# A fused cosine attention and FFN: first loads and head preparation in a hand-chosen order, permuted token order, W3 transposes two ahead

## The chip, the cores and the metric

The kernel runs on one core of a Trainium2 chip. The metric is the device time of one execution in microseconds (us). A profile's span, from the first to the last instruction, is 1.7 to 2.5 us shorter than the time of the same execution.

## The reference, cut to what matters

Eight batches, twelve heads, 448 tokens, head size 64. q and k are divided by their norms, the scores by tau = 0.1, then softmax and the product with v. The result, 3584 x 768, goes through an FFN.

```python
q_n = q / (np.linalg.norm(q, axis=-1, keepdims=True) + 1e-06)
k_n = k / (np.linalg.norm(k, axis=-1, keepdims=True) + 1e-06)
scores = np.matmul(q_n, k_n.transpose(0, 1, 3, 2)) / tau
...                                    # softmax, then attn @ v
h = (x @ w1) * (x @ w2) @ w3
return (h @ w_out)
```

The kernel computes W34 = W3 @ W_out once, for which W3 is transposed on TensorE ("w3t" groups), and then needs only (x W1 * x W2) W34.

## The kernel before

Heads are prepared in groups of six (three pairs). A step t is half a pair: scores and exponentials of pair t/2, attention times v of the pair before, and "filler" groups of FFN matmuls that keep TensorE full. The program order is kept on each engine (in the trace before, the first scaling, whose norms were ready at 8.2 us, stands on POOL until 22.04 behind a load's issue that waited 9.27). In the code `nc.vector` is DVE, `nc.gpsimd` POOL, `nc.scalar` ACT, `nc.tensor` PE. In the profile `raw` is q and k as loaded, `sq` their squares, `ss` the sums of squares, `rt` and `rn` the norm and its reciprocal, `nrm` the scaled q and k, `qkT` (or `qT`, `kT`) their transposes, `sc` the scores. An a-group or b-group is the six matmuls of one block of x W1 or x W2, whose input is `xT`.

```python
def prep_sq(g, i, eng):            # squares, 112x512 for q and for k of pair i
    ...
def prep_sum(g, i):                # nc.vector.reduce_sum, for q and for k
    ...
def prep_rn(g, i0=0, i1=GP):       # rn = 1 / (sqrt(ss) + eps)
    ...
    nc.vector.tensor_scalar_max(t, ss, TINY)
    nc.scalar.activation(t, t, ACT.Ln)
    nc.scalar.activation(t, t, ACT.Exp, scale=0.5)
    nc.vector.tensor_scalar_add(t, t, NORM_EPS)
    nc.vector.reciprocal(rns[g][:, :, sl, :, 0], t)

def tr(pp):
    ...                            # eight transposes into one PSUM tile
    nc.vector.tensor_copy(kts[pp], ps[:, 1, :S])
    nc.vector.tensor_copy(qts[pp].rearrange("p (t j) -> p j t", j=NJ),
                          ps[:, 0, :S].rearrange("p (j t) -> p j t", j=NJ))
...
load_qk(0, 0, 2); load_qk(0, 2, GH); load_v(0); load_w(w3_sb, moe_w3)   # lines joined
load_qk(1); load_w(wo_sb, moe_w_out); load_v(1)
load_w(w1_sb, moe_w1); load_w(w2_sb, moe_w2); load_qk(2)      # all on nc.gpsimd, with a cast
prep_sq(0, 0, nc.vector); prep_sum(0, 0); prep_rn(0, 0, 1); prep_scale(0, 0, nc.gpsimd)
tr(0)
...
def prep_step(s, g):               # steady state: s = step within the group
    ...                            # loads two and three groups ahead, V copy on nc.gpsimd
    n = g + 2
    if n < NG:
        if s < GP:           prep_sq(n, s, nc.gpsimd)
        if 1 <= s <= GP:     prep_sum(n, s - 1)
        if s == GP + 1:      prep_rn(n)
    n = g + 1
    if n < NG and s >= GP:   prep_scale(n, s - GP, nc.gpsimd)

fill += [w3t_group(fo) for fo in range(KO2)]
fill += [w34_group(fo, mh) for fo in range(KO2) for mh in range(2)]
for t in range(2 * NP + 5):
    pp, half = divmod(t, 2)
    scores(pp, half)
    ...                            # trback(pp - 2) in even steps, tr(pp + 1) in odd ones
    if pp >= 1: filler()
    av(pp - 1, half)
    if pp >= 1: filler()
    prep_step(s, g)
```

## Time and profile before

| | before |
|---|---|
| time, median (lowest to highest) | 451.69 us (451.24 to 451.75, four runs; the profiled one 450.96) |
| span of the profiled run | 448.6 us |
| PE busy | 389.9 us |
| first scores | 26.23 us |
| end of the last copy to the end | 445.1 to 448.6 us |

In the page's list of groups the columns are: line, engine, operation, output and input, count, then busy time, mean ns of one, and the idle time before with its releaser. These rows carry the preparation and the two copies that the change merges:

```profile
L121 POOL TENSOR_TENSOR sq<-raw 112x512 bf16<-112x512 bf16 x90 | 91.5, 1041 | 55.3 <-DVE ss L128 47.7
L146 POOL TENSOR_TENSOR nrm<-raw,rn 112x512 bf16<-112x512 bf16 x96 | 96.8, 1044 | 44.4 <-DVE rn L140 44.4
L166 DVE COPY qT<-ps_tr 128x448 bf16<-128x448 bf16 x48 | 55.2, 1150 | 0.0
L165 DVE COPY kT<-ps_tr 128x448 bf16<-128x448 bf16 x48 | 17.7, 368 | 30.8 <-PE ps_tr L159 30.8
```

Squares and scalings are nearly all on POOL. POOL's squares wait 47.7 us in all for VectorE's sums to free their buffers. Even so POOL has long rows in the first 100 us, one of them the seven instructions that will matter below (four squares, V copy, two squares). A max of VectorE's falls into it and takes 2.02 us, where the max has a median of 0.18:

```profile
83.36 4.03 POOL L121 TENSOR_TENSOR sq<-raw 112x512 bf16<-112x512 bf16 x4
87.34 1.46 POOL L109 COPY v_sb<-vraw 112x1536 bf16<-112x1536 bf16 x1
87.82 2.02 DVE L136 TENSOR_SCALAR rt<-ss 112x48 f32<-112x48 f32 x1
88.76 2.03 POOL L121 TENSOR_TENSOR sq<-raw 112x512 bf16<-112x512 bf16 x2
```

### The profile page before, as it was taken

Reading aid. Unit: us, or ns where it says so; the run is one execution under the profiler, and the core shown is the slowest. Engines: PE = TensorE matmul, PEld = TensorE weight load, DVE = VectorE, ACT = ScalarE, POOL = GpSimd, SP = SyncE. Lnnn points to the kernel's source line nnn. Section 1 sums busy time; section 2 is a strip of 40 time slices with the busy share of each in tenths; the row PEclk is TensorE's granted clock in tenths of the full one; section 3 lists DMA queues with packets and bytes.
Section 4 is the critical chain, followed back from the end, with each engine's and each line's share of the span. In section 5 each row is a group of like instructions: output and inputs, shape, how many; then the busy total and the mean of one; then the engine's idle time right before and its main releaser. Section 6 shows DMA issues by size and latency. Waiting matters only on the chain.

```text
span 448.6 us, 9291 instructions
## 1 busy us (share of the span) xinstructions
PE 389.9 (87%) x3904; PEld 228.6 (51%) x3904; DVE 276.6 (62%) x605; ACT 215.8 (48%) x319; POOL 253.6 (57%) x265
## 2 busy tenths in 40 slices
PE   0030579989999999999998999999989999999996
PEld 0010456655555555655565556555655565556553
DVE  2055397877685868576858685768576855564321
ACT  1011334345655565556556655565566555554121
POOL 9148499986767676757676767576747150000000
PEclk9999879999999999999999999999999999999999
DMA  8999916715062706280718071907130011001003
GB/s 108 208 207 213 200 16 91 94 15 81 4 92 77 122 4 91 82 154 2 94 72 129 0 94 72 164 1 94 72 67 1 1 72 72 1 1 72 35 1 140
DMA packets 40776, 34.92 MB, mean 78 GB/s; under 512 B 1312, under 2 KB 34592, under 8 KB 40736
## 3 DMA queue, kind: packets, MB, share of 16 engines
q0 software_dynamic: 36704, 23.33, 37.1%
q1 hardware_dynamic: 4032, 11.01, 6.4%
q8 instruction: 30, 0.49, 0.5%
q14 instruction: 10, 0.08, 0.1%
HBM read 46.66 MB, written 11.01 MB: 129 GB/s over the span
## 4 chain that ended last, share of the span: by engine, by line
PE 80%; DMA 10%; DVE 7%; POOL 1%; issue 0%; ACT 0%; POOLq 0%; ACTq 0%
PE ps_o L220 16%; PE ps_b L220 16%; PE ps_a L220 16%; PE ps_av L193 10%; PE sc L177 10%; DMA raw<-in_k_dram 7%; PE ps_tr L159 5%; PE ps_w L220 4%; DMA w_sb<-in_moe_w_dram 4%; PE ps_tb L211 3%; DVE ss L128 2%; DVE qT L166 1%; DVE w3t_sb L227 1%; DVE osd L202 1%; POOL raw L98 1%; DVE rt L136 1%
## 5 line engine op out<-in xcount | busy, mean ns | idle before, releaser
L184 ACT ACTIVATE expT<-sc 112x896 bf16<-112x896 f32 x192 | 165.4, 914 | 99.6 <-PE sc L177 99.6
L121 POOL TENSOR_TENSOR sq<-raw 112x512 bf16<-112x512 bf16 x90 | 91.5, 1041 | 55.3 <-DVE ss L128 47.7
L146 POOL TENSOR_TENSOR nrm<-raw,rn 112x512 bf16<-112x512 bf16 x96 | 96.8, 1044 | 44.4 <-DVE rn L140 44.4
L220 PEld LDWEIGHTS <-w_sb 128*128 128x128 bf16 x768 | 68.6, 97 | 49.9
L220 PE MATMUL ps_a<-xT,w_sb 128*128 128x448 bf16 x384 | 83.8, 352 | 0.6 <-DVE xT L214 0.3
L220 PE MATMUL ps_b<-xT,w_sb 128*128 128x448 bf16 x384 | 83.1, 352 | 0.0
L220 PE MATMUL ps_o<-w_sb,abT 128*128 128x384 bf16 x448 | 80.8, 326 | 0.0
L177 PE MATMUL sc<-qT,kT 64*112 64x448 bf16 x384 | 58.2, 380 | 23.7 <-DVE qT L166 16.3
L193 PEld LDWEIGHTS <-expT 112*128 112x128 bf16 x1536 | 62.9, 99 | 15.8 <-issue 1.7
L128 DVE TENSOR_REDUCE ss<-sq 112x8 f32<-112x512 bf16 x96 | 61.3, 677 | 14.6 <-POOL sq L121 14.6
L193 PE MATMUL ps_av<-v_sb,expT 112*128 112x65 bf16 x1536 | 66.2, 195 | 0.0
L258 DVE TENSOR_TENSOR abT<-a_sb,ps_b 128x448 bf16<-128x448 bf16 x64 | 39.7, 621 | 37.1 <-PE ps_b L220 34.4
L166 DVE COPY qT<-ps_tr 128x448 bf16<-128x448 bf16 x48 | 55.2, 1150 | 0.0
L220 PEld LDWEIGHTS <-abT 128*128 128x128 bf16 x448 | 41.0, 98 | 23.3 <-issue 0.3
L159 PE MATMUL ps_tr<-ident,nrm 112*128 112x112 bf16 x384 | 28.3, 217 | 23.6 <-POOL nrm L146 23.6
L177 PEld LDWEIGHTS <-kT 64*112 64x112 bf16 x384 | 17.9, 127 | 56.5 <-issue 24.0
L202 DVE TENSOR_TENSOR osd<-ps_av,rs 128x256 bf16<-128x256 f32 x96 | 40.7, 424 | 3.8
L247 ACT CAST a_sb<-ps_a 128x448 bf16<-128x448 f32 x64 | 34.1, 534 | 17.5 <-PE ps_a L220 15.5
L159 PEld LDWEIGHTS <-nrm 112*128 112x128 bf16 x384 | 20.1, 99 | 40.0 <-POOL nrm L146 24.7
L275 ACT COPY out_sb<-ps_o 128x384 f32<-128x384 f32 x28 | 13.4, 479 | 54.4 <-PE ps_o L220 54.4
L165 DVE COPY kT<-ps_tr 128x448 bf16<-128x448 bf16 x48 | 17.7, 368 | 30.8 <-PE ps_tr L159 30.8
L201 DVE RECIPROCAL rs<-ps_av 128x4 f32<-128x4 f32 x96 | 17.7, 185 | 25.7 <-PE ps_av L193 25.7
(30 smaller groups left out, 222.9 us busy)
## 6 DMA issues: line engine op xcount, KB each, us to landing
out_dram<-out_sb SPq DMA_DIRECT2D x28, 384.0 KB, 2.3
vraw<-in_v_dram POOLq DMA_DIRECT2D x16, 336.0 KB, 7.3
raw<-in_q_dram POOLq DMA_DIRECT2D x15, 336.0 KB, 5.0
raw<-in_k_dram POOLq DMA_DIRECT2D x15, 336.0 KB, 6.8
w_sb<-in_moe_w_dram POOLq DMA_DIRECT2D x2, 1536.0 KB, 35.1
w_sb<-in_moe_w_dram POOLq DMA_DIRECT2D x1, 2048.0 KB, 15.7
wo_sb<-in_moe_w_out_dram POOLq DMA_DIRECT2D x1, 1536.0 KB, 24.3
raw<-in_q_dram POOLq DMA_DIRECT2D x1, 224.0 KB, 4.8
```

What stands on the lines that cost most here:

```text
L121: eng.tensor_mul(s.rearrange("p h j d -> p (h j d)"), x, x)
L128: nc.vector.reduce_sum(sss[g][:, t, 2 * i:2 * i + 2, :], sqs.pop((g, i, t)), axis=AX.X)
L146: eng.tensor_mul(nrms[g][:, i, t].rearrange("p j h d -> p h j d"), raws[g][:, t, 2 * i:2 * i + 2], rns[g][:, t, 2 * i:2 * i + 2].to_broadc ...
L159: nc.tensor.transpose(ps[:, t, j * P:(j + 1) * P], n[:, i, t, j].rearrange("p h d -> p (h d)"), ident[:P, :P])
L166: nc.vector.tensor_copy(qts[pp].rearrange("p (t j) -> p j t", j=NJ), ps[:, 0, :S].rearrange("p (j t) -> p j t", j=NJ))
L177: nc.tensor.matmul(sc[:P, hh, :S], kts[pp][64 * hh:64 * hh + 64, c * P:(c + 1) * P], qts[pp][64 * hh:64 * hh + 64, :], start=True, stop=True)
L184: nc.scalar.activation(exps[pp][:, c], sc[:P, :, :S], ACT.Exp, scale=1.0 / float(tau))
L193: nc.tensor.matmul(ps[:, m, :], exps[pp][:, c, hh, q0:q0 + 128], vt[:, 2 * i + hh, c, :], start=(c == 0), stop=(c == NJ - 1))
L202: nc.vector.tensor_mul(osds[pp][:, :, hh, :], ps[:, :, :D], rs.to_broadcast([128, NJ, D]))
L220: nc.tensor.matmul(o, l, r, start=(i == 0), stop=(i == len(pairs) - 1))
L247: nc.scalar.copy(a_sbs[b, fo], ps[:, :S])
L258: nc.vector.tensor_mul(abts[b // 2][:, fo, c0:c0 + S], a_sbs.pop((b, fo)), ps[:, :S])
```

## The change

Its intent is to start TensorE earlier and to take work off VectorE. The first pair's q and k come as fp32 through the SP and ACT queues; the loads stand in one order; groups 0 to 3 are prepared in hand-placed steps, spread over VectorE, ScalarE and GpSimd; steps 0 to 4 have no fillers, step 5 has ten; token order stays permuted until the stores; a W3 transpose is issued two groups ahead of its use. The buffer of W3 is also used again for the FFN's product. Cut to the core:

```diff
-        nc.vector.tensor_copy(kts[pp], ps[:, 1, :S])
-        nc.vector.tensor_copy(
-            qts[pp].rearrange("p (t j) -> p j t", j=NJ),
-            ps[:, 0, :S].rearrange("p (j t) -> p j t", j=NJ))
+        qks[pp] = head_pool.tile([128, 2, S], BF16, tag="qkT", name="qkT")
+        nc.vector.tensor_copy(qks[pp], ps[:, :, :S])
...
+            nc.sync.dma_start(out=out_v[2 * bb + bj // NJ, bj % NJ, p0:p0 + n],
+                              in_=o[r0:r0 + n])          # up to two stores a block
...
+    nc.sync.dma_start(out=raw0[:, 0], in_=q[0, 0:2]...)    # fp32
+    nc.scalar.dma_start(out=raw0[:, 1], in_=k[0, 0:2]...)
...
+    load_qk(0, 2, GH)
...
+    load_w(w3_sb, moe_w3, 0, KO2 // 2)
+    load_v(0)
+    load_w(wo_sb, moe_w_out, 0, KO2)
+    load_qk(1); load_v(1)
...
+    load_w(w3_sb, moe_w3, KO2 // 2, KO2)
+    load_w(w1_sb, moe_w1, 0, KO1)
...
+    fill += [w3t_group(0), w3t_group(1)]
+    for fo in range(KO2):
+        fill.append(w34_group(fo, 0))
+        if fo + 2 < KO2:
+            fill.append(w3t_group(fo + 2))
+        fill.append(w34_group(fo, 1))
+    NFILL0 = 10
...
+        if t == 4:
+            prep_sq(1, 0, 0, DVE);  prep_sq(1, 0, 1, DVE)
+            prep_sq(1, 1, 0, POOL); prep_sq(1, 1, 1, POOL)
+            prep_sum(1, 0, 0); prep_sum(1, 0, 1)
+            prep_max(1, 0, 1); prep_root(1, 0, 1); prep_rn(1, 0, 1)
+            prep_scale(1, 0, 0, DVE); prep_scale(1, 0, 1, DVE)
+        if t == 5:
+            prep_sq(1, 2, 0, POOL); prep_sq(1, 2, 1, POOL)
+            spread_v(1)
+        if t == 6:
+            ...                        # four sums, max, root, rn, then scalings on POOL
...                                    # group 2 in steps 9 to 11, group 3 in 12 to 14
+        if t == 5:
+            av(1, 1)
+            filler(NFILL0)
```

More of the change, by code (lines that the diff above doesn't have):

```diff
@@ L62 @@
     xpool = ctx.enter_context(tc.tile_pool(name="xt", bufs=2))
-    ab_pool = ctx.enter_context(tc.tile_pool(name="ab", bufs=2))
+    ab_pool = ctx.enter_context(tc.tile_pool(name="ab", bufs=1))
     opool = ctx.enter_context(tc.tile_pool(name="opool", bufs=3))
@@ L69 @@
     psM = ctx.enter_context(tc.tile_pool(name="psM", bufs=2, space=PSUM))
-    nc.scalar.preload_act_table_set("natural_log_exp_and_others")
-    ident = const.tile([128, 128], BF16)
-    make_identity(nc, ident)
     w1_sb = wpool.tile([128, KO1, DF], BF16, name="w1_sb")
@@ L78 @@
     w34_sb = wpool.tile([128, KO2, DM], BF16, name="w34_sb")
-    w3_sb = wpool.tile([128, KO2, DF], BF16, name="w3_sb")
     w3t_sb = wpool.tile([128, KO2, DF], BF16, name="w3t_sb")
     wo_sb = wpool.tile([128, KO2, DM], BF16, name="wo_sb")
+    w3_sb = ab_pool.tile([128, KO2, DF], BF16, tag="big", name="w3_sb")
     NV = 3
     v_tiles = [wpool.tile([P, GH, NJ, D + 1], BF16, name=f"v{i}_sb") for i in range(NV)]
-    for t in v_tiles:
-        nc.gpsimd.memset(t[:, :, :, D:D + 1], 1.0)
     raws, vraws, nrms, rns, sss = {}, {}, {}, {}, {}
@@ L106, in load_v, with raw_of, load_w @@
             out=vraws[g], in_=v[b, hb:hb + GH].rearrange("h (p j) d -> p h j d", j=NJ))
+    def raw_of(g, t, i):
+        if (g, i) == (0, 0):
+            return raw0[:, t]
+        return raws[g][:, t, 2 * i:2 * i + 2]
     def spread_v(g):
         nc.gpsimd.tensor_copy(v_tiles[g % NV][:, :, :, :D], vraws.pop(g))
-    def load_w(t, w):
-        nc.gpsimd.dma_start(out=t, in_=w.rearrange("(ko p) n -> p ko n", p=128))
+    def load_w(t, w, k0, k1):
+        nc.gpsimd.dma_start(out=t[:, k0:k1],
+                            in_=w.rearrange("(ko p) n -> p ko n", p=128)[:, k0:k1])
@@ L114, with prep_sq @@
     sqs = {}
-    def prep_sq(g, i, eng):
-        r = raws[g]
-        for t in range(2):
-            s = sq_pool.tile([P, 2, NJ, D], BF16, tag="sq", name="sq", bufs=6)
-            x = r[:, t, 2 * i:2 * i + 2].rearrange("p h j d -> p (h j d)")
-            eng.tensor_mul(s.rearrange("p h j d -> p (h j d)"), x, x)
-            sqs[g, i, t] = s
-    def prep_sum(g, i):
+    def prep_sq(g, i, t, eng):
+        s = sq_pool.tile([P, 2, NJ, D], BF16, tag="sq", name="sq", bufs=6)
+        x = raw_of(g, t, i).rearrange("p h j d -> p (h j d)")
+        o = s.rearrange("p h j d -> p (h j d)")
+        if eng is nc.scalar:
+            eng.activation(o, x, ACT.Square)
+        else:
+            eng.tensor_mul(o, x, x)
+        sqs[g, i, t] = s
@@ L125, in prep_sum, with rn_of @@
+    def prep_sum(g, i, t):
         if g not in sss:
             sss[g] = st_pool.tile([P, 2, GH, NJ], FP32, tag="ss", name="ss")
-        for t in range(2):
-            nc.vector.reduce_sum(sss[g][:, t, 2 * i:2 * i + 2, :], sqs.pop((g, i, t)), axis=AX.X)
-    def prep_rn(g, i0=0, i1=GP):
-        sl = slice(2 * i0, 2 * i1)
+        nc.vector.reduce_sum(sss[g][:, t, 2 * i:2 * i + 2, :], sqs.pop((g, i, t)), axis=AX.X)
+    def rn_of(g, i0, i1):
         if g not in rns:
             rns[g] = st_pool.tile([P, 2, GH, NJ, 1], FP32, tag="rn", name="rn")
-            rns[g, 't'] = st_pool.tile([P, 2, GH, NJ], FP32, tag="rt", name="rt")
-        t, ss = rns[g, 't'][:, :, sl, :], sss[g][:, :, sl, :]
+            rns[g, "t"] = st_pool.tile([P, 2, GH, NJ], FP32, tag="rt", name="rt")
+        sl = slice(2 * i0, 2 * i1)
+        return rns[g, "t"][:, :, sl, :], sss[g][:, :, sl, :], rns[g][:, :, sl, :, 0]
@@ L136, in prep_rn, with prep_max, prep_root @@
+    def prep_max(g, i0=0, i1=GP):
+        t, ss, _ = rn_of(g, i0, i1)
         nc.vector.tensor_scalar_max(t, ss, TINY)
+    def prep_root(g, i0=0, i1=GP):
+        t, _, _ = rn_of(g, i0, i1)
         nc.scalar.activation(t, t, ACT.Ln)
         nc.scalar.activation(t, t, ACT.Exp, scale=0.5)
+    def prep_rn(g, i0=0, i1=GP):
+        t, _, rn = rn_of(g, i0, i1)
         nc.vector.tensor_scalar_add(t, t, NORM_EPS)
-        nc.vector.reciprocal(rns[g][:, :, sl, :, 0], t)
-    def prep_scale(g, i, eng):
+        nc.vector.reciprocal(rn, t)
@@ L143, in prep_scale @@
+    def prep_scale(g, i, t, eng):
         if g not in nrms:
             nrms[g] = nrm_pool.tile([P, GP, 2, NJ, 2, D], BF16, tag="nrm", name="nrm")
-        for t in range(2):
-            eng.tensor_mul(
-                nrms[g][:, i, t].rearrange("p j h d -> p h j d"),
-                raws[g][:, t, 2 * i:2 * i + 2],
-                rns[g][:, t, 2 * i:2 * i + 2].to_broadcast([P, 2, NJ, D]))
-    qts, kts, exps, avs, osds, xts = {}, {}, {}, {}, {}, {}
+        eng.tensor_mul(
+            nrms[g][:, i, t].rearrange("p j h d -> p h j d"),
+            raw_of(g, t, i),
+            rns[g][:, t, 2 * i:2 * i + 2].to_broadcast([P, 2, NJ, D]))
@@ L153, in tr @@
+    qks, exps, osds, xts = {}, {}, {}, {}
     def tr(pp):
@@ L162, in tr, with scores @@
                     ident[:P, :P])
-        qts[pp] = head_pool.tile([128, S], BF16, tag="qT", name="qT")
-        kts[pp] = head_pool.tile([128, S], BF16, tag="kT", name="kT")
-        nc.vector.tensor_copy(kts[pp], ps[:, 1, :S])
-        nc.vector.tensor_copy(
-            qts[pp].rearrange("p (t j) -> p j t", j=NJ),
-            ps[:, 0, :S].rearrange("p (j t) -> p j t", j=NJ))
-    def scores(pp, half):
+        qks[pp] = head_pool.tile([128, 2, S], BF16, tag="qkT", name="qkT")
+        nc.vector.tensor_copy(qks[pp], ps[:, :, :S])
+    def scores(pp, half, between=None):
         if half == 0:
@@ L178, in scores @@
                     sc[:P, hh, :S],
-                    kts[pp][64 * hh:64 * hh + 64, c * P:(c + 1) * P],
-                    qts[pp][64 * hh:64 * hh + 64, :],
+                    qks[pp][64 * hh:64 * hh + 64, 1, c * P:(c + 1) * P],
+                    qks[pp][64 * hh:64 * hh + 64, 0, :],
                     start=True, stop=True)
@@ L185, in scores @@
                                  scale=1.0 / float(tau))
+            if between is not None and c % 2 == 0:
+                between()
     def av(pp, hh):
@@ L252, in f @@
             if b % 2 == 0 and fo == 0:
-                abts[b // 2] = ab_pool.tile([128, KO2, 2 * S], BF16, tag="abT", name="abT", bufs=1)
+                abts[b // 2] = ab_pool.tile([128, KO2, 2 * S], BF16, tag="big", name="abT")
             ps = psM.tile([128, 512], FP32, tag="pm", name="ps_b")
@@ L261, with store @@
     osbs = {}
+    out_v = out.rearrange("(b p j) n -> b j p n", p=P, j=NJ)
+    def store(bb, ch, o):
+        c0 = ch * 128
+        while c0 < ch * 128 + 128:
+            bj, p0 = divmod(c0, P)
+            n = min(P - p0, ch * 128 + 128 - c0)
+            r0 = c0 - ch * 128
+            nc.sync.dma_start(out=out_v[2 * bb + bj // NJ, bj % NJ, p0:p0 + n],
+                              in_=o[r0:r0 + n])
+            c0 += n
     def out_group(bb, ch, mh):
@@ L275, in f @@
                 nc.scalar.copy(o[:, NH:], ps[:, :NH])
-                r0 = bb * 2 * S + ch * 128
-                nc.sync.dma_start(out=out[r0:r0 + 128, :], in_=osbs.pop((bb, ch)))
+                store(bb, ch, osbs.pop((bb, ch)))
         return f
@@ L293, in filler @@
                 fill.pop(0)()
-    load_qk(0, 0, 2)
+    DVE, POOL, SCA = nc.vector, nc.gpsimd, nc.scalar
+    raw0 = raw_pool.tile([P, 2, 2, NJ, D], FP32, tag="raw0", name="raw0", bufs=1)
+    nc.sync.dma_start(out=raw0[:, 0], in_=q[0, 0:2].rearrange("h (p j) d -> p h j d", j=NJ))
+    nc.scalar.dma_start(out=raw0[:, 1], in_=k[0, 0:2].rearrange("h (p j) d -> p h j d", j=NJ))
+    nc.scalar.preload_act_table_set("natural_log_exp_and_others")
     load_qk(0, 2, GH)
+    ident = const.tile([128, 128], BF16)
+    make_identity(nc, ident)
+    load_w(w3_sb, moe_w3, 0, KO2 // 2)
     load_v(0)
-    load_w(w3_sb, moe_w3)
+    load_w(wo_sb, moe_w_out, 0, KO2)
     load_qk(1)
-    load_w(wo_sb, moe_w_out)
     load_v(1)
-    load_w(w1_sb, moe_w1)
-    load_w(w2_sb, moe_w2)
-    load_qk(2)
-    prep_sq(0, 0, nc.vector)
-    prep_sum(0, 0)
+    for t in v_tiles:
+        POOL.memset(t[:, :, :, D:D + 1], 1.0)
+    load_w(w3_sb, moe_w3, KO2 // 2, KO2)
+    load_w(w1_sb, moe_w1, 0, KO1)
+    prep_sq(0, 0, 0, DVE)
+    prep_sq(0, 0, 1, SCA)
+    prep_sum(0, 0, 0)
+    prep_sum(0, 0, 1)
+    prep_max(0, 0, 1)
+    prep_root(0, 0, 1)
+    prep_sq(0, 1, 0, DVE)
+    prep_sq(0, 1, 1, SCA)
+    prep_sq(0, 2, 0, SCA)
+    prep_sq(0, 2, 1, SCA)
     prep_rn(0, 0, 1)
-    prep_scale(0, 0, nc.gpsimd)
+    prep_scale(0, 0, 0, DVE)
+    prep_scale(0, 0, 1, DVE)
     tr(0)
-    spread_v(0)
-    prep_sq(0, 1, nc.vector)
-    prep_sq(0, 2, nc.vector)
-    prep_sum(0, 1)
-    prep_sum(0, 2)
-    prep_rn(0, 1, GP)
-    prep_scale(0, 1, nc.gpsimd)
-    prep_scale(0, 2, nc.gpsimd)
+    prep_sum(0, 1, 0)
+    prep_sum(0, 1, 1)
+    prep_max(0, 1, 2)
+    fill = []
+    def filler(n=1):
+        for _ in range(n):
+            if fill:
+                fill.pop(0)()
+    fill += [w3t_group(0), w3t_group(1)]
[5 more added lines that the diff above has]
+    NFILL0 = 10
     def prep_step(s, g):
@@ L329, in prep_step @@
             if s < GP:
-                prep_sq(n, s, nc.gpsimd)
+                prep_sq(n, s, 0, POOL)
+                prep_sq(n, s, 1, POOL)
             if 1 <= s <= GP:
-                prep_sum(n, s - 1)
+                prep_sum(n, s - 1, 0)
+                prep_sum(n, s - 1, 1)
             if s == GP + 1:
+                prep_max(n)
+                prep_root(n)
                 prep_rn(n)
@@ L336, in prep_step, with first @@
         if n < NG and s >= GP:
-            prep_scale(n, s - GP, nc.gpsimd)
-    fill += [w3t_group(fo) for fo in range(KO2)]
-    fill += [w34_group(fo, mh) for fo in range(KO2) for mh in range(2)]
-    started = False
+            prep_scale(n, s - GP, 0, POOL)
+            prep_scale(n, s - GP, 1, POOL)
+    def first(t):
+        if t == 0:
+            prep_rn(0, 1, 2)
+            prep_scale(0, 1, 0, POOL)
+            prep_scale(0, 1, 1, DVE)
+            load_qk(2)
+            spread_v(0)
+            prep_sum(0, 2, 0)
+        if t == 1:
+            prep_sum(0, 2, 1)
+            prep_max(0, 2, 3)
+        if t == 2:
+            prep_rn(0, 2, 3)
+            prep_scale(0, 2, 0, POOL)
+            prep_scale(0, 2, 1, DVE)
+            load_w(w2_sb, moe_w2, 0, KO1)
+            load_v(2)
+        if t == 4:
+            prep_sq(1, 0, 0, DVE)
+            prep_sq(1, 0, 1, DVE)
+            prep_sq(1, 1, 0, POOL)
+            prep_sq(1, 1, 1, POOL)
+            prep_sum(1, 0, 0)
+            prep_sum(1, 0, 1)
+            prep_max(1, 0, 1)
+            prep_root(1, 0, 1)
+            prep_rn(1, 0, 1)
+            prep_scale(1, 0, 0, DVE)
+            prep_scale(1, 0, 1, DVE)
+        if t == 5:
+            prep_sq(1, 2, 0, POOL)
+            prep_sq(1, 2, 1, POOL)
+            spread_v(1)
+        if t == 6:
+            for i in (1, 2):
+                prep_sum(1, i, 0)
+                prep_sum(1, i, 1)
+            prep_max(1, 1, 3)
+            prep_root(1, 1, 3)
+            prep_rn(1, 1, 3)
+            prep_scale(1, 1, 0, POOL)
+            prep_scale(1, 1, 1, POOL)
+        if t == 7:
+            prep_scale(1, 2, 0, POOL)
+            prep_scale(1, 2, 1, POOL)
+            load_qk(3)
+        if t == 8:
+            load_v(3)
+        if t == 9:
+            prep_sq(2, 0, 0, DVE)
+            prep_sq(2, 0, 1, DVE)
+            for i in (1, 2):
+                prep_sq(2, i, 0, POOL)
+                prep_sq(2, i, 1, POOL)
+            prep_sum(2, 0, 0)
+            prep_sum(2, 0, 1)
+        if t == 10:
+            prep_max(2, 0, 1)
+            prep_root(2, 0, 1)
+            prep_rn(2, 0, 1)
+            prep_scale(2, 0, 0, DVE)
+            prep_scale(2, 0, 1, DVE)
+            load_qk(4)
+        if t == 11:
+            for i in (1, 2):
+                prep_sum(2, i, 0)
+                prep_sum(2, i, 1)
+            prep_max(2, 1, 3)
+            prep_root(2, 1, 3)
+            prep_rn(2, 1, 3)
+            prep_scale(2, 1, 0, POOL)
+            prep_scale(2, 1, 1, POOL)
@@ new lines, in second, with prep @@
+    def second(s):
+        if s == 0:
+            spread_v(2)
+            prep_scale(2, 2, 0, POOL)
+            prep_scale(2, 2, 1, POOL)
+        if s < GP:
+            prep_sq(3, s, 0, DVE)
+            prep_sq(3, s, 1, DVE)
+            prep_sum(3, s, 0)
+            prep_sum(3, s, 1)
+        if s == GP - 1:
+            prep_max(3)
+            prep_root(3)
+            prep_rn(3)
+    def prep(t):
+        g, s = divmod(t, 2 * GP)
+        if g < 2:
+            first(t)
+        else:
+            if g == 2:
+                second(s)
+            prep_step(s, g)
@@ L343 @@
     for t in range(2 * NP + 5):
         pp, half = divmod(t, 2)
+        mid = {0: lambda: prep_root(0, 1, 2), 2: lambda: prep_root(0, 2, 3)}.get(t)
         if pp < NP:
-            scores(pp, half)
+            scores(pp, half, mid)
         if half == 0 and 0 <= pp - 2 < NP:
@@ L350 @@
                 fill += ffn_groups((pp - 2) // NPAIR)
+        if t == 5:
+            av(1, 1)
+            filler(NFILL0)
         if half == 1 and pp + 1 < NP:
             tr(pp + 1)
-        if t == 0:
-            for i in range(GP):
-                prep_sq(1, i, nc.gpsimd)
-                prep_sum(1, i)
-            prep_rn(1)
-        if pp >= 1:
+        if pp >= GP:
             filler()
-        if 0 <= pp - 1 < NP:
+        if 0 <= pp - 1 < NP and t != 5:
             av(pp - 1, half)
-        if pp >= 1:
+        if pp >= GP:
             filler()
         if pp < NP:
-            g, s = divmod(t, 2 * GP)
-            prep_step(s, g)
+            prep(t)
     while fill:
```

## The prediction

The terms for a cold clock, 2.5 us in step 5 and 2 in step 7, were estimates.

> **What bounds the kernel now.** I read the page's slices first, then busy time by window, then the timeline of the first 110 us and of one later batch, then the waits. The slices:
>
> ```profile
> PE   0030579989999999999998999999989999999996
> DMA  8999916715062706280718071907130011001003
> ```
>
> One slice is 11.2 us. TensorE is full from about 70 us to the end. Before that it mostly waits, while the DMA row is full for five slices. By window (columns: length, busy time and count of PE, PEld, DVE, ACT, POOL, then clock, DMA share, GB/s):
>
> ```profile
> 15.00:20.00 5.00, 0.00 (x0) 0.00 (x0) 0.00 (x0) 0.00 (x0) 0.00 (x0) 1.00 1.12 213
> 50.00:55.00 5.00, 0.36 (x4) 0.36 (x4) 2.35 (x5) 0.66 (x1) 3.81 (x4) 0.70 1.45 197
> 150.00:200.00 50.00, 50.00 (x517) 28.96 (x516) 36.06 (x80) 29.01 (x43) 34.41 (x35) 1.00 0.49 84
> ```
>
> PE busy is 389.9 of 448.6 us, so 58.7 us are idle: about 54.7 before or between work, 4.0 in the tail. Only some 4 us of this lie between 109 us and the tail. The rest is the start, and the change is about the start. What happens there, from the timeline:
>
> ```profile
> 11.20 0.78 POOL L98 DMA_DIRECT2D raw<-in_q_dram  x1 [0.23 <-DMA vraw<-in_v_dram]
> 21.25 0.77 POOL L98 DMA_DIRECT2D raw<-in_k_dram  x1 [9.27 <-DMA w_sb<-in_moe_w_dram]
> 22.04 2.05 POOL L146 TENSOR_TENSOR nrm<-raw,rn 112x512 bf16<-112x512 bf16 x2
> 26.23 0.99 PE L177 MATMUL sc<-qT,kT 64*112 64x448 bf16 x4 [1.54 <-DVE qT L166]
> 50.48 1.04 POOL L121 TENSOR_TENSOR sq<-raw 112x512 bf16<-112x512 bf16 x1 [6.95 <-DMA raw<-in_q_dram]
> ```
>
> The norms of the first pair were ready at 8.2 us, but the scaling stands on POOL behind a DMA issue that waited 9.3 us for w3. In both issues that waited, the transfer waited for is the one eight software issues earlier. Later POOL's queue stands before group 2's squares until 50.5 us because that load is the last of 9.6 MB. So the first scores come at 26.2 us. The loop (two steps t to a pair of heads) starts step 6, the scores of pair 3, at 66.55, and step 14, where the FFN of batch 0 begins, at 101.18; step 16 starts at 109.11 (these starts are read from PE's timeline, before the end of its records of the step). And in the steady part:
>
> ```profile
> 144.90 1.15 DVE L166 COPY qT<-ps_tr 128x448 bf16<-128x448 bf16 x1
> 146.10 0.58 PE L177 MATMUL sc<-qT,kT 64*112 64x448 bf16 x4 [1.03 <-DVE rs L201]
> 147.63 0.38 DVE L214 COPY xT<-ps_tb 128x448 bf16<-128x448 bf16 x1
> ```
>
> In a step with no FFN group to fill it, PE waits for VectorE. That happens about once in two batches.
>
> [...] The permuting qT copy took 1150 ns[...]. [...] the granted clock is 0.50 in 55 to 60. [...]
>
> **The change part by part.** *Copies.* Token order stays permuted, so kT (0.37) and qT (1.15) become one copy of 0.60: 0.92 us of DVE per pair, 44 us in all, nearly all beside a full PE. In a step without a filler it lets the next scores start earlier, but two sums (1.27) and the xT copy still stand before the last a-matmul, so I count 0.4 us, three times: 1.2 us off the path. The stores become up to two DMAs per block: 0.2 us at the tail.
>
> *First pair.* SP and ACT load fp32 at about 0.8 us, landing about 3.3 (28 stores took 2.3 us to land). Then square 0.69, two sums 1.3, max 0.17, Ln and Exp 0.43, add and reciprocal 0.43, scaling 1.4, with a square of q0b waiting between (landing about 6.5); transposes and the copy 1.6. First scores at about 10 us, 16 earlier.
>
> *Steps 0 to 5.* No fillers. Loads now set step 5. I add fp32 bytes read in the new order and look them up on the old curve (1.95 MB by 10 us, 4.0 by 15, 6.1 by 20, 8.1 by 25, 10.2 by 30; from the windows' GB/s doubled), 0.8 us earlier because POOL issues earlier, plus 0.6 seen between curve and landing. Up to k of group 1 it is 8.7 MB: 26 us. Then VectorE does step 4's chain for group 1: square 0.4, sums 1.3, max and root 0.7, reciprocal 0.45, scaling 1.4 (contention aside): 30.3. Only behind it come osd (0.6) and w3t's first eviction (0.7). So the ten fillers of step 5 really begin at 31.6: eight remaining groups, five of 1.30 and three of 0.45, make 7.9 us, with 2.5 for a cold clock and 1.2 for transposes and copy. Step 6 starts at 43.5 instead of 66.5: 23 us won.
>
> *Steps 6 to 13: where part is given back.* Preparation of groups 1, 2 and 3, which the old kernel had mostly behind it, now lies here, and much of it on VectorE. At step 6 four sums (2.65) stand after the second filler's eviction (0.76), then max 0.2, root 0.5, rn 0.55, and two POOL scalings (2.05): 6.7 us after that filler, while PE has only scores (0.5) to do. The transposes of step 7 come before its fillers, so PE waits 5 to 6 us and cools (2 us). At step 11 the same form with step 10's chain and step 9's backlog: 3.5 us. Step 13 has no filler (24 groups: ten, then seven steps of two). There VectorE has 15 us queued from step 11's last eviction to the xT copy of block 5: step 11's prep 3.9, step 12's xT, evictions, osd and prep 4.3, step 13's 3.4, sums of group 4 with 1.3, and a wait of about 2 for their squares, as POOL has scalings, a spread (1.47), loads (2.4) and squares in front. PE has 3.3 us of work in this time beside two fillers: some 9 us idle. PE's own work in steps 6 to 13 is 14 fillers (15.7) and eight steps of 1.48 (11.8): 27.5, against 32.6 before, whose steps had 16 fillers. Adding up: 43.5 + 27.5 + 5.5 + 2 + 3.5 + the part of the 9 us before step 14 (about 4) gives step 14 at 86. The first a-group then ends at 92 to 93 instead of 103.6, and step 14's VectorE chain (4.3 to 4.7) costs step 16 some 2 to 3 us more: step 16 at about 100 to 101.5, instead of 109.1.
>
> *Sum.* 109.1 - 100.8 = 8.3; with 1.2 for the steady part and minus 0.2 for the tail, 9.3 us: 442.4. My walk lets every in-order queue wait fully and takes the clock as cold twice (4.5 us). The floor for steps 6 to 15 is VectorE's own work: base 11, evictions 8.2, abT 1.2, preparation 22.2, together 42.6 us, so step 16 could not come before 43.5 + 43 = 86.5 (23.8 us won with the rest, 428). I take the walk with a fifth of the distance to the floor: 439.5.
>
> **The rivals.** (1) The whole start-up gain stays: 23 us at step 6 reach the end, about 428. For it: PE, once fed, runs full, and someone who chose this order by hand will have seen most waits. Against it: the placement of four sums before the transposes' scalings is in the program, and VectorE is already at 8.9 of 10 us in 80 to 90 before. (2) The loads bound anyway: nothing but DMA order changes, and w1, w2 land near 40 and 50 us. Against it: the FFN first needs them at 86, so they hide; if the fillers waited for wo and w3 until 35, it would cost 3 us: 443. (3) Steady state gains much from 44 us less VectorE work, some 5 us more: 434. Against it: PE is busy 50.00 of 50 us in 150 to 200. (4) VectorE and POOL contend in the crowded steps and 15 us more are lost: the time stays at 450.
>
> **Range and chances.** The walk's uncertain terms: landing of group 1 (2 us), cold clock (4), the three stalls (6 together). From the floor to a bad walk: 430 to 447. 2% faster is 442.66; with the middle at 439.5 and about 6 us of spread, I give 0.70 for faster and 0.29 for within. Slower by 9 us would need the later part to lose, where nothing is added.
>
> **What would show it.** Right: first scores near 10 us; step 6 near 43; a PE wait of 5 us or so for POOL's nrm just after, and one before the first full a-group with VectorE's sums in front; 150 to 200 still full; one 0.6 us copy for qk. Wrong: step 7's transposes without a wait, or step 16 under 95 (then under 436); k of group 1 landing after 30 (then over 443); stores taking longer at the end.

## More of the kernel before

The "V copy" is POOL's COPY v_sb<-vraw, one for each group.

A "row" of POOL is a chain of its instructions without a pause, and a "hold" is a VectorE instruction that takes far longer than others of its form and shape.

## The result, and the profile after

The changed kernel takes 457.54 us (457.01 to 458.55, four runs) against 451.69: slower by 1.3%, which is under 2% but clear of the noise. The ratio is 1.0134 with a 95% interval of 1.0116 to 1.0153. Ratios here are the mean time of one kernel's fast runs over that of the other's of the same rounds, so not quite the ratio of the medians. The prediction was 439.5, range 430 to 447: outside, and with the wrong sign.

TensorE is busy from the first slice now, but with holes up to the eleventh, and its granted clock is reduced in six slices:

```profile
PE   1547677678499999999999999999999999999995
PEclk9996979958889999999999999999999999999999
```

The starts of the steps in PE's timeline say where the time went (walk: the prediction's; the walk gives no step 18 or 20, so the old kernel's lengths are put in):

| step | before | walk | after |
|---|---|---|---|
| 0 | 26.23 | 10 | 10.58 |
| 6 | 66.55 | 43.5 | 49.55 |
| 14 | 101.18 | 86 | 91.64 |
| 16 | 109.11 | 100.8 | 106.84 |
| 18 | 116.55 | 108.2 | 122.40 |
| 20 | 123.98 | 115.7 | 132.35 |
| span | 448.6 | 439.3 | 455.7 |

At step 16 the changed kernel is still 2.3 us ahead. By step 20 it is 8.4 us behind, and the rest wins back 1.3 us. (The two profiled spans differ by 7.1 us, the medians of the times by 5.9.) Two stretches are wrong against the walk: before step 6, and between 16 and 20. The timeline of the changed kernel at the first:

```profile
26.39 4.03 POOL L122 TENSOR_TENSOR sq<-raw 112x512 bf16<-112x512 bf16 x4
26.57 5.87 DVE L122 TENSOR_TENSOR sq<-raw 112x512 bf16<-112x512 bf16 x2
30.38 1.46 POOL L107 COPY v_sb<-vraw 112x1536 bf16<-112x1536 bf16 x1
37.37 2.74 PE L226 MATMUL ps_w<-wo_sb,w3t_sb 128*128 128x384 bf16 x8 [9.08 <-DVE w3t_sb L233]
```

Two squares on VectorE, 0.42 us each when alone, take 5.87 us together: the first 5.54, to 32.11, and the second 0.41. The first ends 0.3 us after POOL's unbroken row of four squares and a V copy ends (31.84). It is not data: POOL's own four squares, k's among them, ran at full speed from 26.4, and they read the same load. The fillers then start 6 us later than in the walk, on a reduced clock (granted 0.50 in 37 to 40 us: 2.74 for a group that takes 1.46 at a granted clock of 1.00). At the second stretch:

```profile
113.72 7.66 DVE L148 TENSOR_SCALAR rt<-rt 112x48 f32<-112x48 f32 x1 [0.58 <-ACT rt L144]
113.90 4.03 POOL L122 TENSOR_TENSOR sq<-raw 112x512 bf16<-112x512 bf16 x4
117.88 1.46 POOL L107 COPY v_sb<-vraw 112x1536 bf16<-112x1536 bf16 x1
119.31 2.03 POOL L122 TENSOR_TENSOR sq<-raw 112x512 bf16<-112x512 bf16 x2
122.40 0.99 PE L181 MATMUL sc<-qkT 64*112 64x448 bf16 x4 [6.45 <-DVE qkT L172]
123.73 2.45 PE L226 MATMUL ps_a<-xT,w_sb 128*128 128x448 bf16 x6
```

An add of 48 numbers per partition, 0.19 us by its median, takes 7.66 us and ends when POOL's seven instructions end. The qk copy stands behind it, PE waits 6.45 us for that copy, and what PE does next runs at a granted clock of 0.50 (mean of 122 to 125 us; an a-group of 1.30 takes 2.45). A mean would hide this: the 20 adds have a median of 0.19 and a maximum of 7.66.

The waits that the prediction did foresee are there too, at step 7 for POOL's scalings (named in the prediction, 5 to 6 us) and at step 14 for the xT copy:

```profile
59.07 0.55 PE L167 MATMUL ps_tr<-ident,nrm 112*128 112x112 bf16 x4 [4.97 <-POOL nrm L154]
97.52 0.53 PE L226 MATMUL ps_a<-xT,w_sb 128*128 128x448 bf16 x1 [2.48 <-DVE xT L220]
```

The copy is as computed (before: the rows of qT and kT above):

```profile
L172 DVE COPY qkT<-ps_tr 128x896 bf16<-128x896 bf16 x48 | 29.1, 606 | 20.7 <-PE ps_tr L167 20.7
```

### The profile page after: what moved, and what is told of

Read it like the earlier page. It is cut to its first block, busy times and chain, and to the rows that moved or that the text cites. A ratio compares the mean times of both kernels' runs of the same rounds, so it can differ in the third digit from the quotient of the medians.

```text
span 455.7 us, 9284 instructions
## 1 busy us (share of the span) xinstructions
PE 400.5 (88%) x3904; PEld 233.0 (51%) x3904; DVE 265.5 (58%) x580; ACT 218.9 (48%) x329; POOL 236.2 (52%) x246
## 4 chain that ended last, share of the span: by engine, by line
PE 80%; DVE 10%; POOL 4%; DMA 3%; ACT 2%; issue 1%; DVEq 0%; ACTq 0%; POOLq 0%
PE ps_o L226 16%; PE ps_a L226 16%; PE ps_b L226 16%; PE ps_av L199 10%; PE sc L181 9%; PE ps_tr L167 4%; PE ps_w L226 4%; PE ps_tb L217 3%; DMA vraw<-in_v_dram 3%; DVE ss L128 2%; DVE rt L148 2%; POOL nrm L154 2%; DVE sq L122 2%; ACT expT L188 1%; DVE w_sb L242 1%
## 5 line engine op out<-in xcount | busy, mean ns | idle before, releaser
L154 POOL TENSOR_TENSOR nrm<-raw,rn 112x512 bf16<-112x512 bf16 x88 | 90.0, 1056 | 87.3 <-DVE rn L149 87.3
L122 POOL TENSOR_TENSOR sq<-raw 112x512 bf16<-112x512 bf16 x80 | 81.3, 1039 | 41.5 <-DVE ss L128 41.3
L226 PEld LDWEIGHTS <-w_sb 128*128 128x128 bf16 x768 | 70.0, 99 | 52.3 <-issue 4.0
L226 PE MATMUL ps_a<-xT,w_sb 128*128 128x448 bf16 x384 | 86.9, 363 | 2.5 <-DVE xT L220 2.5
L226 PE MATMUL ps_b<-xT,w_sb 128*128 128x448 bf16 x384 | 84.4, 356 | 0.0
L181 PE MATMUL sc<-qkT 64*112 64x448 bf16 x384 | 60.4, 388 | 16.7 <-DVE qkT L172 14.3
L199 PEld LDWEIGHTS <-expT 112*128 112x128 bf16 x1536 | 64.0, 100 | 19.7 <-issue 6.0
L181 PEld LDWEIGHTS <-qkT 64*112 64x112 bf16 x384 | 18.8, 129 | 50.3 <-issue 23.9
L172 DVE COPY qkT<-ps_tr 128x896 bf16<-128x896 bf16 x48 | 29.1, 606 | 20.7 <-PE ps_tr L167 20.7
L293 ACT COPY out_sb<-ps_o 128x384 f32<-128x384 f32 x28 | 13.4, 479 | 54.4 <-PE ps_o L226 54.4
L226 PE MATMUL ps_w<-wo_sb,w3t_sb 128*128 128x384 bf16 x128 | 25.6, 350 | 9.3 <-DVE w3t_sb L233 9.1
```

The costliest lines, as they stand in the source:

```text
L122: eng.tensor_mul(o, x, x)
L154: eng.tensor_mul(nrms[g][:, i, t].rearrange("p j h d -> p h j d"), raw_of(g, t, i), rns[g][:, t, 2 * i:2 * i + 2].to_broadcast([P, 2, NJ, D]))
L172: nc.vector.tensor_copy(qks[pp], ps[:, :, :S])
L181: nc.tensor.matmul(sc[:P, hh, :S], qks[pp][64 * hh:64 * hh + 64, 1, c * P:(c + 1) * P], qks[pp][64 * hh:64 * hh + 64, 0, :], start=True, s ...
L199: nc.tensor.matmul(ps[:, m, :], exps[pp][:, c, hh, q0:q0 + 128], vt[:, 2 * i + hh, c, :], start=(c == 0), stop=(c == NJ - 1))
L226: nc.tensor.matmul(o, l, r, start=(i == 0), stop=(i == len(pairs) - 1))
```

## The experiments

**Theory A**: some VectorE instructions are held as long as GpSimd runs without a break, and this made both stretches. **B**: the add waits for data or a semaphore, or VectorE is simply overloaded. **C** for the first stretch: k of group 1 lands late. All kernels gave correct results. Times are medians; "the kernel before" took 451.3 to 451.8 in the same rounds.

**1. The norm's reciprocal on ScalarE, for every group.**

```diff
-        nc.scalar.activation(t, t, ACT.Exp, scale=0.5)
-        nc.vector.tensor_scalar_add(t, t, NORM_EPS)
-        nc.vector.reciprocal(rn, t)
+        nc.scalar.activation(rn, t, ACT.Exp, scale=-0.5)
```

> The changed kernel with 1/norm made on ScalarE as Exp(-0.5 Ln) for every group: no add and no reciprocal on VectorE. Theory A (VectorE instructions [...] are held for as long as GpSimd runs without a break): the 7.66 us TENSOR_SCALAR at 113.7 is gone, the 6.45 us wait of the scores at 122.4 and the cold clock behind it too, so 8 to 11 us less: 447 to 449. Rival B (that TENSOR_SCALAR waits for data or a semaphore of GpSimd's squares, or VectorE is simply behind): what follows is held in its place and only about 0.6 us a group is won: 456 to 457.

Measured 444.11 us (ratio 0.9827, 0.9800 to 0.9854). Step 18 starts at 109.04 instead of 122.40, and the wait of 6.45 us is gone:

```profile
109.04 0.59 PE L179 MATMUL sc<-qkT 64*112 64x448 bf16 x4
109.80 1.30 PE L224 MATMUL ps_a<-xT,w_sb 128*128 128x448 bf16 x6
```

Steps 16 to 20 take 15.19 us instead of 25.51. The total is more than expected, because step 6 came 2.5 us earlier too and steps 6 to 16 took 54.2 us instead of 57.3. B falls, for its 0.6 us a group were to leave 456 or more.

**2. Group 1's squares on ScalarE.**

```diff
-            prep_sq(1, 0, 0, DVE);  prep_sq(1, 0, 1, DVE)
-            prep_sq(1, 1, 0, POOL); prep_sq(1, 1, 1, POOL)   # and (1, 2, .) in step 5
+            prep_sq(1, 0, 0, SCA);  prep_sq(1, 0, 1, SCA)
+            prep_sq(1, 1, 0, SCA);  prep_sq(1, 1, 1, SCA)    # and (1, 2, .) in step 5
```

> The changed kernel with all six squares of group 1 on ScalarE in place of VectorE and GpSimd. Theory A: VectorE's chain of step 4 no longer stands 5 us at its squares beside GpSimd's stream (26.6 to 32.4); step 6 starts at about 44 to 45 instead of 49.5; the end 3 to 6 us earlier unless the later hold (113.7) grows. Rival C (k of group 1 lands only at about 32): step 6 stays at 49 to 50, the time at 457.

Measured 452.25 us (1.0013). Step 6 starts at 44.34. C falls: the loads were there at 26. The later hold is untouched and as long as before, five microseconds earlier; and a hold on the add of pair 3 ends with the V copy that was left (27.91 to 29.38):

```profile
28.27 1.14 DVE L148 TENSOR_SCALAR rt<-rt 112x16 f32<-112x16 f32 x1 [0.53 <-ACT rt L144]
108.47 7.65 DVE L148 TENSOR_SCALAR rt<-rt 112x48 f32<-112x48 f32 x1 [0.58 <-ACT rt L144]
```

**3. Both edits.**

> Both edits together. Theory A: gains add up, 12 to 16 us less than 457.5, so 442 to 446. Rivals B and C: 456 to 457.

Measured 440.42 us (0.9754, 0.9729 to 0.9778). The gains nearly add up: 13.4 and 5.3 alone, 17.1 together, some 2 us more than expected.

**4. Only the permuted order, in the kernel before.** The diff is the copy and the stores of the change, nothing else.

> The kernel before with only the permuted token order: one qk copy of 0.6 us and the stores in up to two parts. From the two traces: three fillerless steps gain about 0.8 us each, the tail loses 1.0 us (451.2 to 455.7 against 445.1 to 448.6), the crowded first 100 us may gain up to 3 us as VectorE has 0.9 us less a pair: 447 to 451. If the permuted stores cost in the steady part (rival), it is over 452.

Measured 448.07 us (0.9924, 0.9910 to 0.9938), as expected. So this part of the change is good for 3.4 us, and the rest of the change cost some 9.5 us (448.07 to 457.54, from two different sets of rounds).

**5. The stream taken away, the held instruction left.**

```diff
-                prep_sq(n, s, 0, POOL); prep_sq(n, s, 1, POOL)
+                prep_sq(n, s, 0, SCA if n == 5 else POOL)
+                prep_sq(n, s, 1, SCA if n == 5 else POOL)
```

> The changed kernel, VectorE's add left as it is, and only group 5's six squares moved from GpSimd to ScalarE: this takes the stream away and leaves the instruction that was held. Theory A: the add of group 4, 7.66 us before, takes at most about 1.7 us (GpSimd's V copy of 1.47 is still there), step 18 comes at about 112 to 114, the time is 447 to 450. If the add itself were the cause (too many VectorE instructions), it stays long or something else is in its place, and the time stays at 456 to 458.

The add is where it was and POOL has only its V copy beside it:

```profile
113.17 1.69 DVE L148 TENSOR_SCALAR rt<-rt 112x48 f32<-112x48 f32 x1 [0.58 <-ACT rt L144]
113.33 1.48 POOL L107 COPY v_sb<-vraw 112x1536 bf16<-112x1536 bf16 x1
115.88 0.59 PE L181 MATMUL sc<-qkT 64*112 64x448 bf16 x4 [0.44 <-DVE qkT L172]
```

This is the cleanest evidence on the add: the hold shrinks from 7.66 to 1.69 us, the end of the V copy, and PE's wait from 6.45 to 0.44. Step 18 comes at 115.88, later than my 112 to 114. The time is 451.49 us by its median, the profiled run 448.47, the other three 451.4 to 452.2. My range of 447 to 450 holds only the profiled one. Only the profiled one has a trace, so where these 3 us lie is open.

**6. Control: the edit of run 1 in the kernel before.**

> Control: the same 1/norm on ScalarE in the kernel before. Its only held instruction over 1 us is the max of 2.02 us at 87.8, which stays, and the add's holds there are 0.2 us each. Theory A: 449.5 to 451.5, so the 13 us of the first run are particular to the changed order. If 0.6 us a group less VectorE work were what helps: 440 to 445.

Measured 448.75 us (0.9937, 0.9922 to 0.9952): 2.8 us less, just past my 449.5 to 451.5. I had expected the max's hold of 2.02 us to stay; in this run the same max, at 87.35, took 0.62 us. It started 0.5 us earlier. So the same instruction can take 2.02 us or 0.62. The edit was worth 2.8 us here and 13.4 in the changed kernel.

**7. Group 1's other two pairs prepared inside step 5's fillers.** On top of run 3 (the squares of the last pair also move up, from step 5 to 4):

```diff
         if t == 5:
             av(1, 1)
-            filler(NFILL0)
+            filler(4)
+            spread_v(1)
+            ...            # sums, max and root of pairs 4 and 5, their scalings on POOL
+            filler(NFILL0 - 4)
```

> The two edits together, and the sums, norms and scalings of pairs 4 and 5 moved from the end of step 6 into the middle of step 5's fillers. My reading of the wait in step 7 (four sums, root, scaling stand between the second filler of step 6 and the transposes): the wait of 4.4 us and the cold clock behind it go, step 8 starts at 52 to 53 instead of 58.2; the end gains 3 to 6 us if the later waits do not take it: 434 to 438. Rival: VectorE is full from step 8 to 14 anyway and the gain ends there: 439 to 441.

Measured 432.85 us (0.9592, 0.9576 to 0.9609). Step 8 starts at 51.74 instead of 58.24 in run 3, 6.5 us earlier, and the gain reaches the end: 7.6 us, more than expected. The prediction's reading of that wait was right.

**8. Groups 2 and 3 two to three steps earlier**, on top of run 7. Pair 6 and group 3 have their squares on ScalarE, pairs 7 and 8 on GpSimd; pair 6's scalings go from VectorE to GpSimd.

```diff
-        if t == 9:  ...   # squares of group 2      (10, 11: norms, scalings)
+        if t == 7:  ...   #                         (8, 9)
-            if g == 2: second(s)          # group 3 in steps 12 to 14
+        if t >= 9: second(t - 9)          # in steps 9 to 11
```

> As the run before it, and the preparation of groups 2 and 3 two to three steps earlier, with the squares of pair 6 and of group 3 on ScalarE. The waits of step 11 (2.1), 14 (2.7 and 2.6) should shrink: step 16 at 90 to 94, the time 428 to 434, if VectorE has room in steps 7 to 11; if GpSimd's streams hold VectorE's max of group 2 or 3 it is 435 to 438.

Measured 429.05 us (0.9506, 0.9490 to 0.9522); step 16 at 87.84, earlier than expected. Of the holds that were left, the two after step 6 were both on the max (1.95 and 2.09 us), the first of them beside a V copy and squares of POOL:

```profile
74.30 1.95 DVE L139 TENSOR_SCALAR rt<-ss 112x48 f32<-112x48 f32 x1
74.64 1.46 POOL L107 COPY v_sb<-vraw 112x1536 bf16<-112x1536 bf16 x1
76.06 2.08 POOL L122 TENSOR_TENSOR sq<-raw 112x512 bf16<-112x512 bf16 x2
```

This hold ends with the copy, not with the squares behind it.

**9. Only the add left out of the changed kernel.**

```diff
-        nc.vector.tensor_scalar_add(t, t, NORM_EPS)
```

> The changed kernel with only VectorE's add of 1e-6 left out (the norm is 0.8, so the result is the same within rounding); the reciprocal stays on VectorE and now stands first behind the root, in the middle of GpSimd's stream. Theory A in its narrow form (only instructions of certain forms are held: the fp32 tensor_scalar and the products of two SBUF operands, not the reciprocal or the reductions, which never took over 0.46 and 0.69 us): the reciprocal takes 0.45 us, no hold of 7 us, time 444 to 449. Wide form (any VectorE instruction on SBUF is held): the reciprocal takes 7 us and the time stays at 456 to 458.

Measured 445.74 us (0.9900, 0.9868 to 0.9931). The gain is most of run 1's. But the question of the two forms was missed: without the add the reciprocal ran at 109.99, ahead of POOL's row, which began at 111.90.

**10. The max out too**, on top of run 8:

```diff
-        nc.vector.tensor_scalar_max(t, ss, TINY)
-        nc.scalar.activation(t, t, ACT.Ln)
+        nc.scalar.activation(t, ss, ACT.Ln, bias=tiny[:P])
```

> The fastest so far with VectorE's max taken out too (its constant is added inside ScalarE's Ln): the two holds of 1.95 and 2.09 us at 74 and 92 go. Theory A: 1 to 4 us less than 429.0, so 425 to 428. If PE's waits there are set by ScalarE's order instead, 428.5 to 429.5.

Measured 423.76 us (0.9383, 0.9363 to 0.9402, five runs): 5.3 us less than run 8, more than my 1 to 4. It is the fastest kernel of this study, 6.2% under the kernel before and some 7% under the changed one (423.76 against 457.54). TensorE after it:

```profile
PE   1648998999999999999999999999999999999995
PEclk9997999999999999999999999999999999999998
```

**11. The last store's second part from ScalarE's queue.**

```diff
-            nc.sync.dma_start(...)
+            q = nc.scalar if (bb, ch) == (B // 2 - 1, 6) and r0 > 0 else nc.sync
+            q.dma_start(...)
```

> The run before it, and the second part of the very last store issued by ScalarE's queue instead of after the first part on SyncE. If the 1.0 us longer tail of the permuted stores is the second issue standing behind the first: 0.5 to 1.0 us less than the run before. If it is the transfer itself, no difference.

Measured 424.34 us against 423.76: no gain. The tail's extra microsecond is not the second issue standing behind the first. What it is stays open.

**12. The reciprocal moved into POOL's row.** As run 9, with the reciprocal one step later:

```diff
-            if s == GP + 1: prep_max(n); prep_root(n); prep_rn(n)
+            if s == GP + 1: prep_max(n); prep_root(n)
+            if s == GP + 2: prep_rn(n)
```

> The changed kernel without the add, and the reciprocal of groups 4 and later one step later, so that for group 4 it falls into GpSimd's stream of squares, V copy, squares (in the run without the add it fell just ahead of it). Only the row of that reciprocal counts. Narrow form of theory A: 0.45 us inside the stream. Wide form: several us, up to the stream's end.

One look, 447.24 us (a single execution, state unknown; only this stretch counts). The row it was made for:

```profile
114.27 4.03 POOL L122 TENSOR_TENSOR sq<-raw 112x512 bf16<-112x512 bf16 x4
114.86 0.62 DVE L263 TENSOR_TENSOR abT<-a_sb,ps_b 128x448 bf16<-128x448 bf16 x1 [0.57 <-PE ps_b L225]
115.40 0.45 DVE L148 RECIPROCAL rn<-rt 112x48 f32<-112x48 f32 x1
```

The reciprocal, fp32 in SBUF like the add, takes 0.45 us in the middle of POOL's squares, and so does the product with one operand in PSUM take its usual 0.62. VectorE's sums, which read their squares from SBUF, took at most 0.69 us in both kernels (96 in each). So the narrow form of theory A holds in this: which instructions were held depended on their form, not on VectorE touching SBUF. But of the products of two SBUF operands only the squares were held. The changed kernel's scalings on VectorE took 0.68 to 0.69 us; beside two of them it was GpSimd's scaling that took longer, 1.54 and 1.55 us instead of 1.04.

## Why the prediction was wrong, point by point

**The step that failed** is the overlap of VectorE with GpSimd, which the prediction counts as free: it leaves "contention aside" in step 4's chain, names it in its fourth rival and adds nothing for it. Against the walk's span (448.6 less its 9.3 us, so 439.3) three stretches are longer: 6.0 us before step 6, where the squares are held, 8.1 between steps 16 and 18, where the add is held, 2.5 between 18 and 20, the reduced clock behind it (0.50 in 122 to 125 us, 0.54 in 125 to 128). That is 16.6. With 1.1 more won in the steady part and 0.8 more lost in the tail than I put in, 439.3 + 16.6 - 1.1 + 0.8 = 455.6, and the span is 455.7. The stretches are differences from the walk; what the holds made of them, the runs show. Run 2 brings step 6 forward by 5.2 of the 6.0 us, and run 1 takes 10.3 of the other 10.6 out of steps 16 to 20. The prediction also said that a slower kernel would need the later part to lose, "where nothing is added"; steps 16 to 20 are where it lost.

**The fourth rival was the true one.** It said that VectorE and GpSimd contend in the crowded steps, 15 us more are lost and the time stays at 450. What it named is what the runs show (with POOL's squares beside it moved to ScalarE the add took 1.69 us instead of 7.66, run 5), and its 15 us are near the 16.6. That it named nearly this size was luck, for nothing in it was worked out; and its 450 doesn't follow from the walk, for 442.4 + 15 is 457.4, almost what was measured. I gave it too little because the trace before showed only one hold over 1 us (the max of 2.02 at 87.8), and I had read that row as part of VectorE's load. The sign that I passed over: 15 instructions of one shape with a mean of 347 ns, where the other shapes took 174 to 180.

**Why it was rare before.** It was not for want of rows. The kernel before has the row of seven shown above, and two of 12 and 13 instructions (52.23 to 64.67 and 67.30 to 80.73). Four fp32 tensor_scalars fell into these three rows and took 0.41 to 2.02 us; the max of 2.02 got through while the row went on. In run 8 too a max got through in the middle of a row (1.95 us at 74.30). By the profile's starts, the add of 7.66 us began 0.18 us before its row and the square of 5.54 us 0.18 us after the start of its own; these waited for the whole row. So theory A is too simple as I worded it: some of VectorE's instructions are held beside GpSimd's (7.66 us beside seven of them, 1.69 beside the V copy alone, run 5), but why one is held for a single instruction of GpSimd's and another for a row is explained by no run here.

**First pair: right.** Scores at 10.58 against "about 10"; q was waited for until 4.06, not 3.3.

**Loads: right.** k of group 1 was there when POOL squared it (26.4 to 30.4; walk: 26), and run 2 confirmed it. In both kernels every POOL issue that waited for a transfer waited for the one eight software issues earlier (two and three of them; the longest wait was 9.27 us). What sets this, no run shows.

**Steps 6 to 16: right in sum.** 43.5 to 100.8 is 57.3 us in the walk, 49.55 to 106.84 is 57.3 measured. The wait of step 7 was 4.97 (said: 5 to 6), and run 7 removed it by the means its reading suggests. The wait of step 11 was 2.59 (said: 3.5). That the sum is exact is luck: inside it lies a pair of held squares, 2.37 us at 87.5 instead of 0.84, for which the walk has nothing, so other terms were too long.

**Adjusting the walk toward the floor: wrong.** I moved the result from 442.4 to 439.5 because I took the walk as pessimistic. It lacked a whole class of waits.

**Steady part: mechanism right, size off; tail: size off, cause open.** Steps 25 to 27 took 6.52 us before and 5.76 after, 0.76 three times, so 2.3 us against my 1.2. The tail is 4.5 us instead of 3.5, so 1.0 more against my 0.2, and run 11 shows that the second issue is not what it waits for.

## What to carry to other kernels

Before giving work to GpSimd beside VectorE, list which VectorE instructions are of the forms that were held here, and ask what stands behind them: the bf16 square (5.54 us instead of 0.42), the fp32 add (7.66 instead of 0.19) and the fp32 max (2.02 instead of 0.18). Here a tiny add on the path to TensorE was held for a whole row of GpSimd work. Look at the maximum of a group's durations, not only its mean. Moving the norm's tiny instructions and six squares to ScalarE took 17 us off here (run 3), and the new order, which had lost by itself, then paid. The fair yardstick for run 1 (444.11) is the kernel before with the same edit (448.75, run 6): the order is worth 4.6 us between them, from different rounds.
